# A hand-written planner's cost table and leads, re-measured and re-searched

## The chip, the cores and the metric

One core of one Trainium2 chip. Time is device microseconds of one execution; lower is better. The engines are TensorE (PE; PEld is its weight load), VectorE (DVE), ScalarE (ACT), GpSimd (POOL) and SyncE (SP, which only issues DMAs).

## The reference

Sorted block attention, whose output goes through a Fourier mixing layer with a normalised two-layer MLP. Four batches, 8 heads, 768 rows, 64 columns a head, 8 blocks of 96 rows; the model width is 512 and the MLP's is 2048.

```python
P = sort_net
for _ in range(5):                      # row and column normalisation of exp(P - max)
    ...
k_sorted = einsum('bhij,bhjcd->bhicd', P, k_blocks)     # v_sorted likewise
scores = scale * q_blocks @ k_sorted_blocks^T           # block by block
attn = softmax(scores); x = attn @ v_sorted             # (4, 768, 512)
X = real(fft(fft(x, axis=1), axis=2))
u = x + X
un = (u - mean(u)) / sqrt(var(u) + 1e-6)
out = u + relu(un @ w_ch1) @ w_ch2
```

## The kernel before

The work of one batch b runs through these steps; the names in quotes are those that the planner uses.

- Mixing of the blocks: "load_v" (SyncE) and "load_k16", "load_q16" (GpSimd) bring in a pair of heads. "psQ", "qT" turn q. "kron" makes the mixing matrix, "psK" and "kz" mix k. "psaT", "amr", "amr2", "psA", "a16", "a24" make the column means of v. "psV" mixes v, "vo" takes it from PSUM and subtracts the mean (VectorE, line 692, 8 to a batch), and "v_move" (line 700, 12 to a batch, SyncE) moves the mixed values with a DMA from one layout of partitions into another, `vs`. "a_out" and "a_row" move rows of means (lines 671 and 878).
- Attention, head by head: in batches 0 and 1 "psS" and "max" (line 771) find the maxima, "psT" and "exp" the shifted scores, "minus" takes 1 off in 16 bits, and "twice" (line 850) copies one column. In batches 2 and 3 the maxima come first along the other axis, and "turn_e" turns the result by a DMA. "psN" (line 856) multiplies by the values `vs`; it needs all moves of its half batch. "norm" (lines 862 and 863) divides on VectorE.
- Fourier transform: "fold" (line 882, VectorE or GpSimd) and "fold2" (line 887, VectorE, two instructions) add and subtract quarters of the rows for a pair of heads; "psWe", "psWo" (line 903) and the copies "We", "Wo" are the transform over the rows, "fold_d", "psF", "ot", "P", "Q" that over the columns.
- Sum and norm: "psR", "u", "add" (lines 1007 and 1008, GpSimd), "store_u" (line 1014, SyncE), "stats", "root", "nm", "un"; "psY" and "unT" turn the result on TensorE, or "turn_u" (line 1066) by a DMA in batches 2 and 3.
- MLP, two groups of 384 rows for each batch: "ph" (line 1104, four matmuls each), "relu" (line 1110), "pc" (line 1125, four matmuls each), "load_u" (line 1090, SyncE) brings back the residual, "outt" (line 1133) adds it, "store" (line 1148, GpSimd, indirect) writes the rows out.

Nothing on the chip chooses an order: each engine runs its own instructions in the order in which the program was written, and waits on semaphores. That order is made by the class `Plan` while the program is built. Each operation is a `step` with a duration in ns for every engine that can do it (`{"V": 425, "G": 1450}`), the keys that it reads and writes, and for a DMA its time on the queue (`work`) and until it has landed (`hop`). `run` keeps the list of steps whose predecessors are planned, works out for each when each engine could start it, takes all that could start within 40 ns of the earliest, and of these the one with the lowest priority number. A priority is 1e5 times the batch minus the length of the chain of steps still to come, plus a lead: `LEAD` gives for a step's name four numbers, one for each batch, in us (a negative one moves the step forward, a positive one back). The MLP's steps have priorities behind all of these, and bulk loads ahead of them.

Four of the planner's rules matter here. After a step the engine is taken to be free 60 ns before the step's end on VectorE and ScalarE (the last line of the `emit` part below). A step whose name is in `PORT` isn't started on VectorE while the planner has GpSimd at work, but 450 ns behind that at the latest. Whatever follows a DMA is put 2.5 us behind the time at which the planner has that DMA landed (`SPARE`). And a step that may run on two engines goes to the one that ends it sooner, if both have the same priority and could start within those 40 ns.

```python
        done = at + ns
        if e == "G" and not s.hop:
            self.pool = (at, done)
        self.free[e] = done if e in "TGS" else done - 60.0
```

Of the kernel before, what the change touches and what calls it, by code (L numbers as in the profile page):

```python
# [197 lines left out]
class Plan:  # L198
    HALF, TURNS = ("psQ", "psK", "psaT"), 200
    LAG, PE_TAIL, MARGIN, NEAR = 45.0, 215.0, 120.0, 40.0  # L200
    PORT, PORT_WAIT = ("fold", "fold_d", "minus", "nm", "un", "v_cast"), 450.0
    SPARE = 2500
    LEAD = dict(P=(42.1, 0, 0, 0), Q=(0, 32.3, 0, 0), We=(0, 0.1, 0, -4.3), Wo=(0, 0.1, 0, 0),
        a16=(0, 0, 0, 57.3), a24=(0, -25.2, 0, 0), add=(0, 0, 8.7, 0), amr2=(8.9, 0, 0, -13.1),
        exp=(0, 0, 17.5, 0), fold=(-32.4, 0, 41.2, -24.5), fold2=(-31.2, 0, 0, -34.7), kz=(1.7, 52.5, 0, 0),
        load_k16=(0, -3.8, -1.9, 0), load_q16=(0, -34.2, -1.6, -27.5), max=(54, 0, 0, 0),
        minus=(0, -8, 50.8, 3), psF=(30.4, 3.5, 0, 4.8), psK=(0, 0, 0, 15.9), psR=(7.6, 0, -10, 0),
        psS=(55.3, -5.2, 0, 0), psT=(5.1, -15.7, 0, 0), psWe=(0, 0, 0, 46.1), psY=(2.9, 0, 0, 0),
        psaT=(0, 7.5, 0, 0), stats=(-48, 2.1, 47.9, 0), twice=(0, 2.1, 0, -33.7), v_sum=(0, 0, -13.8, 0),
        vo=(0, -38.1, 0, -28.7))  # L210
    DMA_AHEAD = 800

    def __init__(self, engines):
# [179 lines left out]
def kernel(  # L393
# [108 lines left out]
    def load_v(b, hp, need):  # L502
        v32[b, hp] = Buf("hr" if 4 * b + hp in (0, 1, 2, 3, 7) else "v32")

        def f(e):
            nc.sync.dma_start(v_view(b, hp), v[b, 2 * hp:2 * hp + 2].rearrange(
                "h (p g) d -> p h (g d)", g=G))
# [160 lines left out]
    def a_out(b):  # L668
        def f(e):
            for p, lo, hi, at in ((BLK + 8, 0, 8, 0), (BLK + 9, 0, 7, 1), (BLK + 9, 7, 8, 4)):  # L670
                nc.sync.dma_start(xr2[b % 2][p:p + 1, lo:hi].rearrange("o i m -> o (i m)"),
                                  a16s[b % 2][at:at + hi - lo])
        step("a_out", b, {"S": 2100}, f, r=[("a16", b % 2)], w=[("xa", b % 2)], work=150, hop=1500, lanes=3)

    def row_zero(b):
        def f(e):
# [20 lines left out]
    def v_move(b, half):  # L697
        for g in range(G):
            def f(e, g=g):
                (nc.gpsimd if e == "G" else nc.sync).dma_start(  # L700
                    vs[2 * (b % 2) + half][16 * g:16 * g + 16].rearrange("c i e -> c (i e)"),
                    vo[half][:, g].rearrange("p h e -> p (h e)"))
# [93 lines left out]
    def turned(n):  # L796
# [22 lines left out]
        for y in range(2):  # L819
            es = Buf("es")  # L820

            def g(e, y=y, es=es):
# [6 lines left out]
            step("turn_e", b, {"S": 1250}, lambda e, y=y, es=es: nc.sync.dma_start(  # L829
                et.t[:, 4 * y:4 * y + 4, 0:BLK], es.t.rearrange("q j k -> q (j k)"), transpose=True),  # L830
                r=[es], w=[(et, y)], work=600, hop=1500)

# [11 lines left out]
    def values(n):  # L844
# [3 lines left out]
        def twice(e):  # L848
            row = eT[n].t[0:BLK].rearrange("p i q -> p (i q)")
            plan.engines[e].tensor_copy(row[:, BLK:NB * (BLK + 16):BLK + 17], eT[n].t[0:BLK, :, 0])  # L850
        step("twice", b, {"G": 270, "V": 120}, twice, r=[(eT[n], y) for y in range(2)], w=[(eT[n], 2)])

        def f(e):
            ps = pair(pN, D + 1, BLK + 8)
# [17 lines left out]
    def fold(b, hp):  # L872
# [5 lines left out]
        step("a_row", b, {"S": 600}, lambda e: nc.sync.dma_start(  # L878
            f2.t[BLK + 8:128, 0], a24[b % 2][:, None, ms].broadcast_to([24, 4, 128])),
            r=[("a24", b % 2)], w=[(f2, 0)], work=200, hop=1400)  # L880
        for y, op in enumerate(ops):
            step("fold", b, {"V": 425, "G": 1450}, lambda e, y=y, op=op: plan.engines[e].tensor_tensor(  # L882
                f1.t[:, y], xr[0:BLK + 8, 0:4, ms], xr[0:BLK + 8, 7:3:-1, ms], op=op), r=both, w=[(f1, y)])

        def f(e):
# [113 lines left out]
    def add_res(b, i, m):  # L999
# [4 lines left out]
        def f(e):  # L1004
# [4 lines left out]
        step("add", b, {"G": 1420}, f, r=[lo, hi, u], w=[u])  # L1009
# [49 lines left out]
    def transpose_u(b, i, m):  # L1059
# [3 lines left out]
        if (b, t // 4) not in unT:  # L1063
            unT[b, t // 4] = Buf("unT")
        if b >= 2 and (i, m) != (0, 1):
            step("turn_u", b, {"S": 1250}, lambda e: nc.sync.dma_start(
                unT[b, t // 4].t[:, :, BLK * (t % 4):BLK * (t % 4) + BLK],
                un[b, i, m].t[0:BLK], transpose=True),
                r=[un[b, i, m]], w=[(unT[b, t // 4], t % 4)], work=600, hop=1500)
# [13 lines left out]
    def mlp(b, gr):  # L1083
        hr, ur = {}, {}

        def load_u(t):
            q_ = 3 * gr + t
            ur[t] = Buf("ur")
            r0, r1 = 128 * q_, 128 * q_ + 128
            step("load_u", b, {"S": 430}, lambda e: nc.sync.dma_start(ur[t].t, u_dram[b][r0:r1]),  # L1090
                 r=[("ud", b, j) for j in range(8) if BLK * j < r1 and BLK * j + BLK > r0],
                 w=[ur[t]], work=800, hop=2000, prio=MLP - 1e8)
        MLP = 1e6 + 1e4 * b
# [44 lines left out]
    def store(b, q_, o, prio):  # L1138
        if (b, q_) == (B - 1, 5):
# [8 lines left out]
        step("store", b, {"G": 1020}, lambda e: nc.gpsimd.indirect_dma_start(  # L1148
            out=out.rearrange("b s m -> (b s) m"),
            out_offset=bass.IndirectOffsetOnAxis(ap=idx[:, c:c + 1], axis=0),  # L1150
            in_=o.t, in_offset=None), r=[o, "idx"], work=800, hop=1400, prio=prio)
# [17 lines left out]
        w.gates = (w1sb[0:1, 0, DM * c:DM * c + 1] if i < 4 else w2sb[0:1, 4 * c, 0:1])  # L1169

    def load_const(key, need, t, d):
        step("const", 0, {"S": 400}, lambda e: nc.sync.dma_start(t, d.ap()),
             w=[key], work=6 * int(np.prod(t.shape)) // 1000 + 50, hop=1500, bulk=t.shape[-1] > 1, need=need,
             rel=27000 if key in ("rsel", "idx") else 17500 if key in ("cdh",) else 0.0)

# [189 lines left out]
```

## Time and profile before

| | us |
|---|---|
| median of 3 runs | 324.42 |
| lowest and highest run | 320.97 and 324.87 |
| the profiled execution | 324.41 |
| its span | 322.6 |
| TensorE busy in the span | 285.3 |
| VectorE, ScalarE, GpSimd busy | 224.8, 203.4, 178.3 |

The granted TensorE clock was 0.974 of full speed in the mean. Matmuls are pipelined and their durations overlap, so a busy TensorE needn't be TensorE at its peak. In rows of a timeline stand the start, the length, the engine, the line and the operation with what it writes and reads; "x6" is that many instructions merged. The chain of waits is followed back from the last instruction to whatever released each piece. A wait is put down to what came last by the profile. "SPq" is the sequencer of SyncE, with the time that issuing a DMA takes there.

### The profile page before, as it was taken

How to read it: one execution, taken by the hardware profiler on the slowest of the kernel's cores; microseconds unless marked ns; L12 is line 12 of the kernel's file. 1: busy time of each engine (PE TensorE's matmuls, PEld its weight loads, DVE VectorE, ACT ScalarE, POOL GpSimd, SP SyncE). 2: the span in 40 equal slices, each digit the busy share in tenths (PEclk: the TensorE clock that was granted, in tenths of full speed). 3: DMA queues.
4: the chain of work that ended last, by engine and by line, in shares of the span. 5: the costliest groups of instructions: out<-in, count | busy, mean ns of one | idle time of the engine just before them, and what ended most of it. 6: DMA issues, size and time to landing. Idle time of an engine off the chain costs nothing.

```text
span 322.6 us, 7298 instructions
## 1 busy us (share of the span) xinstructions
PE 285.3 (88%) x2619; PEld 181.4 (56%) x2619; DVE 224.8 (70%) x487; ACT 203.4 (63%) x477; POOL 178.3 (55%) x246
## 2 busy tenths in 40 slices
PE   8877679959868798999999999997999999999990
PEld 5657556946655455555665656653655654645540
DVE  6689867899957989976878998998456764101010
ACT  6567657877746538875888989948832772713500
POOL 8623667849546799994748343975024965212020
PEclk9999966999989999999999999999999999999998
DMA  7952965897489977799997448556533537414021
GB/s 212 174 127 67 227 153 75 123 204 183 114 138 175 183 191 243 138 155 194 158 248 107 107 120 114 151 149 183 145 61 131 160 82 193 113 58 139 0 86 44
DMA packets 56062, 45.38 MB, mean 141 GB/s; under 512 B 25011, under 2 KB 48162, under 8 KB 56026
## 3 DMA queue, kind: packets, MB, share of 16 engines
q1 hardware_dynamic: 41226, 28.35, 34.7%
q0 software_dynamic: 14800, 16.57, 29.5%
q8 instruction: 20, 0.33, 0.4%
q14 instruction: 16, 0.13, 0.2%
HBM read 34.60 MB, written 12.58 MB: 146 GB/s over the span
## 4 chain that ended last, share of the span: by engine, by line
PE 49%; DVE 21%; DMA 12%; issue 6%; POOL 5%; SPq 3%; ACT 2%; POOLq 0%; DVEq 0%; ACTq 0%
PE bank L1104 18%; PE bank L1125 17%; DVE st L1025 3%; DMA vs<-vo 2%; PE bank L856 2%; DMA hr<-in_v_dram 2%; SPq L700 2%; DMA k<-in_k_dram 2%; DVE vo L692 2%; DMA out_dram<-outt,idx_sb 2%; DVE x L887 2%; DMA q<-in_q_dram 2%; PE bank L903 2%; DVE xr L863 2%; DVE kz L493 2%
## 5 line engine op out<-in xcount | busy, mean ns | idle before, releaser
L1104 PE MATMUL bank<-unT,w1sb 128*128 128x384 f16 x512 | 90.8, 328 | 2.2 <-DMA unT<-un 1.5
L1125 PE MATMUL bank<-w2sb,hr 128*128 128x512 f16 x384 | 90.6, 379 | 0.0
L1110 ACT ACTIVATE hr<-bank 128x384 f16<-128x384 f32 x128 | 60.7, 492 | 32.9 <-PE bank L1104 32.0
L1104 PEld LDWEIGHTS <-w1sb 128*128 128x128 f16 x512 | 48.5, 98 | 32.8 <-DMA unT<-un 2.0
L1125 PEld LDWEIGHTS <-hr 128*128 128x128 f16 x384 | 36.0, 98 | 37.5
L1148 POOL DMA_INDIRECT out_dram<-outt,idx_sb x23 | 23.7, 1028 | 55.1 <-DVE outt L1133 31.0
L1133 DVE SCALAR_TENSOR_TENSOR outt<-ur,bank 128x512 f32<-128x512 f32 x24 | 16.5, 686 | 37.9 <-PE bank L1125 37.4
L810 ACT ACTIVATE sm<-bank,mns 96x96 f32<-96x96 f32 x128 | 31.8, 344 | 2.3 <-DVE mns L815 2.2
L882 POOL TENSOR_TENSOR xs<-xr 104x512 f16<-104x512 f16 x13 | 16.1, 1239 | 18.8 <-DVE xr L863 14.0
L856 PE MATMUL bank<-vs,eT 97*104 97x65 f16 x256 | 17.4, 219 | 10.0 <-DMA vs<-vo 3.5
L1025 DVE BATCH_NORM_STATS2 st<-u 96x6 f32<-96x512 f32 (+1 forms) x32 | 21.7, 679 | 5.0 <-POOL u L1008 4.8
L856 PEld LDWEIGHTS <-eT 97*104 97x104 f16 x256 | 16.0, 135 | 14.3 <-issue 5.2
L863 DVE TENSOR_TENSOR xr<-bank,rz 104x512 f16<-104x512 f32 x32 | 22.1, 692 | 1.1
L1053 POOL TENSOR_SCALAR un<-u,mv,rstd 96x512 f16<-96x512 f32 (+1 forms) x8 | 17.0, 2125 | 10.3 <-PE bank L1076 4.1
L487 ACT COPY u<-bank 96x512 f32<-96x512 f32 (+1 forms) x24 | 13.5, 584 | 11.8 <-PE bank L984 6.8
L489 ACT ACTIVATE kz<-bank 64x768 f16<-64x768 f32 x20 | 16.1, 805 | 6.2 <-DVE kz L493 5.8
L887 DVE TENSOR_TENSOR x<-xs 104x512 f16<-104x512 f16 x32 | 16.9, 569 | 3.6 <-POOL xs L882 3.1
L487 ACT CAST W<-bank 128x384 f16<-128x384 f32 (+1 forms) x34 | 11.7, 383 | 10.2 <-PE bank L903 8.9
L815 DVE TENSOR_REDUCE mns<-bank 96x8 f32<-96x768 f32 x16 | 15.1, 946 | 2.0 <-PE bank L805 1.8
L903 PEld LDWEIGHTS <-x 128*128 128x128 f16 (+1 forms) x128 | 10.9, 103 | 9.7 <-DVE x L887 8.3
L692 DVE SCALAR_TENSOR_TENSOR vo<-a,bank 128x384 f16<-128x384 f16 x32 | 16.0, 539 | 0.0
L792 ACT ACTIVATE sm<-bank 96x768 f32<-96x768 f32 x16 | 12.8, 798 | 4.5 <-PE bank L787 4.0
(140 smaller groups left out, 538.6 us busy)
## 6 DMA issues: line engine op xcount, KB each, us to landing
u_dram<-u SPq DMA_DIRECT2D x32, 192.0 KB
ur<-u_dram SPq DMA_DIRECT2D x24, 256.0 KB
v<-in_v_dram SPq DMA_DIRECT2D x11, 384.0 KB
vs<-vo SPq DMA_DIRECT2D x48, 65.0 KB
k<-in_k_dram POOLq DMA_DIRECT2D x15, 192.0 KB, 4.3
q<-in_q_dram POOLq DMA_DIRECT2D x15, 192.0 KB, 5.7
w1sb<-in_moe_w_ch_dram POOLq DMA_DIRECT2D x4, 512.0 KB, 7.8
w2sb<-in_moe_w_ch_dram POOLq DMA_DIRECT2D x4, 512.0 KB, 5.9
```

What stands on the lines that cost most here:

```text
L487: nc.scalar.copy(dst, src)
L692: ("vo", b, {"V": 560}, lambda e: nc.vector.scalar_tensor_tensor(vo[h // 4][:, :, h % 4, 0:D], a16s[b % 2].rearrange("p (h d) -> p h d", d ...
L810: nc.scalar.activation(sm.t[:, i], pair(pS, BLK)[:, y, i % 4], AF.Exp, bias=mn.t[:, i:i + 1], scale=-1.0)
L856: nc.tensor.matmul(ps[:, i // 4, i % 4], eT[n].t[0:97, i, 0:BLK + 8], vs[2 * (b % 2) + h // 4][:, i, (D + 1) * (h % 4):(D + 1) * (h % 4 + 1)])
L863: nc.vector.tensor_tensor(xr2[b % 2][0:BLK + 8, :, D * h:D * (h + 1)].rearrange("p (t j) d -> p t j d", t=2), ps[:, :, :, 0:D], r[:, :, :, ...
L887: nc.vector.tensor_tensor(f2.t[0:BLK + 8, :, 2 * y:2 * y + 2].rearrange("p j f m -> p f j m"), f1.t[:, :, 0:2], f1.t[:, :, 3:1:-1], op=op)
L903: nc.tensor.matmul(ps[:, n * y:n * y + n], f2.t[r, j, xt[y], :], t[r, j, n * y:n * y + n], start=(y == 0 and j == 0), stop=(j == 1), skip_ ...
L1025: nc.vector.bn_stats(st.t[0:n], us[b, i, m].t[0:n])
L1104: nc.tensor.matmul(ps, w1sb[:, mc, 128 * fc:128 * fc + 128], unT[b, gr].t[:, mc, :], start=(mc == 0), stop=(mc == 3))
L1110: nc.scalar.activation(dst, bank(pH, [128, 384]), AF.Relu)
L1125: nc.tensor.matmul(ps, hr[f4].t[:, fc % 4, 128 * t:128 * (t + 1)], w2sb[:, fc, :], start=(fc == 0), stop=(fc == 15))
L1148: step("store", b, {"G": 1020}, lambda e: nc.gpsimd.indirect_dma_start(out=out.rearrange("b s m -> (b s) m"), out_offset=bass.IndirectOffs ...
```

## The change

Only numbers of the planner change, and one rule of it; the operations are the same.

- Durations on SyncE: load_v 400 to 520, a_out 2100 to 2300, v_move 600 to 645, turn_e 1250 to 1300, a_row 600 to 920, store_u 350 to 550, turn_u 1250 to 1310, load_u 430 to 600, constants 400 to 450 ns.
- Durations on GpSimd: twice 270 to 200, fold 1450 to 1160, add 1420 to 1380, store 1020 to 1050 ns.
- The overlap of successive operations, 60 ns for both, becomes 80 on VectorE and 100 on ScalarE.
- fold2 and twice join `PORT`.
- All leads are new.

```diff
-    PORT, PORT_WAIT = ("fold", "fold_d", "minus", "nm", "un", "v_cast"), 450.0
+    PORT, PORT_WAIT = ("fold", "fold2", "twice", "fold_d", "minus", "nm", "un", "v_cast"), 450.0
+    OVER = {"V": 80, "A": 100}
     SPARE = 2500
-    LEAD = dict(P=(42.1, 0, 0, 0), Q=(0, 32.3, 0, 0), We=(0, 0.1, 0, -4.3), Wo=(0, 0.1, 0, 0),
-        a16=(0, 0, 0, 57.3), a24=(0, -25.2, 0, 0), add=(0, 0, 8.7, 0), amr2=(8.9, 0, 0, -13.1),
-        exp=(0, 0, 17.5, 0), fold=(-32.4, 0, 41.2, -24.5), fold2=(-31.2, 0, 0, -34.7), kz=(1.7, 52.5, 0, 0),
-        load_k16=(0, -3.8, -1.9, 0), load_q16=(0, -34.2, -1.6, -27.5), max=(54, 0, 0, 0),
-        minus=(0, -8, 50.8, 3), psF=(30.4, 3.5, 0, 4.8), psK=(0, 0, 0, 15.9), psR=(7.6, 0, -10, 0),
-        psS=(55.3, -5.2, 0, 0), psT=(5.1, -15.7, 0, 0), psWe=(0, 0, 0, 46.1), psY=(2.9, 0, 0, 0),
-        psaT=(0, 7.5, 0, 0), stats=(-48, 2.1, 47.9, 0), twice=(0, 2.1, 0, -33.7), v_sum=(0, 0, -13.8, 0),
-        vo=(0, -38.1, 0, -28.7))
+    LEAD = dict(We=(0, 0, 0, -32.4), Wo=(-26.1, 0, -22, 0), a_row=(0, -15.8, -6.7, -8.5), amr=(0, 0, 0, -24.3),
+        exp=(0, 0, 0, -11.5), fold=(0, -20.3, 0, -26.8), fold2=(0, 0, 0, -6.4), fold_d=(0, 0, -41.8, 0),
+        load_k16=(0, 6, 9.2, 1.9), load_q16=(0, 2.4, 9, 0), load_v=(0, 0, 0, 20.2), max=(0, -0.7, 0, 0),
+        minus=(0, 0, -9.8, -5.4), norm=(60, 0, 0, 0), psR=(0, 14.5, -4.4, 0), psT=(-12.2, 52.1, 0, 0),
+        psV=(0, 0, 0, -14.1), psWo=(-0.9, 0, 0, -20.5), psY=(0, 0, -15.5, 0), stats=(-5, 53.1, 0, 26.5),
+        twice=(14.6, 0, 0, 0), unT=(0, 0, -12.4, 0), v_move=(0, 0, 0, -12.9), vo=(0, 0, -36.6, 0),
+        weights=(-7.7, 0, 0, 0))
...
-        self.free[e] = done if e in "TGS" else done - 60.0
+        self.free[e] = done - self.OVER.get(e, 0.0)
...
-        step("load_v", b, {"S": 400}, f, w=[v32[b, hp]], work=1250, hop=1450, bulk=True, need=need, rel=80000 if b == 2 else 27000 if b == 1 else 0.0)
+        step("load_v", b, {"S": 520}, f, w=[v32[b, hp]], work=1250, hop=1450, bulk=True, need=need, rel=80000 if b == 2 else 27000 if b == 1 else 0.0)
...
-            step("v_move", b, {"S": 600}, f,
+            step("v_move", b, {"S": 645}, f,
...
-        step("a_row", b, {"S": 600}, lambda e: nc.sync.dma_start(
+        step("a_row", b, {"S": 920}, lambda e: nc.sync.dma_start(
...
-            step("fold", b, {"V": 425, "G": 1450}, lambda e, y=y, op=op: plan.engines[e].tensor_tensor(
+            step("fold", b, {"V": 425, "G": 1160}, lambda e, y=y, op=op: plan.engines[e].tensor_tensor(
...
-        step("store_u", b, {"S": 350}, lambda e: nc.sync.dma_start(
+        step("store_u", b, {"S": 550}, lambda e: nc.sync.dma_start(
...
```

More of the change, by code (lines that the diff above doesn't have):

```diff
@@ L672, in f @@
                                   a16s[b % 2][at:at + hi - lo])
-        step("a_out", b, {"S": 2100}, f, r=[("a16", b % 2)], w=[("xa", b % 2)], work=150, hop=1500, lanes=3)
+        step("a_out", b, {"S": 2300}, f, r=[("a16", b % 2)], w=[("xa", b % 2)], work=150, hop=1500, lanes=3)
     def row_zero(b):
@@ L828, in turned @@
             step("minus", b, {"V": 385, "A": 518}, g, r=[(sm, y)], w=[es])
-            step("turn_e", b, {"S": 1250}, lambda e, y=y, es=es: nc.sync.dma_start(
+            step("turn_e", b, {"S": 1300}, lambda e, y=y, es=es: nc.sync.dma_start(
                 et.t[:, 4 * y:4 * y + 4, 0:BLK], es.t.rearrange("q j k -> q (j k)"), transpose=True),
@@ L850, in twice @@
             plan.engines[e].tensor_copy(row[:, BLK:NB * (BLK + 16):BLK + 17], eT[n].t[0:BLK, :, 0])
-        step("twice", b, {"G": 270, "V": 120}, twice, r=[(eT[n], y) for y in range(2)], w=[(eT[n], 2)])
+        step("twice", b, {"G": 200, "V": 120}, twice, r=[(eT[n], y) for y in range(2)], w=[(eT[n], 2)])
         def f(e):
@@ L1008, in f @@
             eng.tensor_tensor(u.t[0:n, LH:DM], u.t[0:n, LH:DM], h[0:n, 255:0:-1], op=ALU.add)
-        step("add", b, {"G": 1420}, f, r=[lo, hi, u], w=[u])
+        step("add", b, {"G": 1380}, f, r=[lo, hi, u], w=[u])
     def store_u(b, i, m):
@@ L1065, in transpose_u @@
         if b >= 2 and (i, m) != (0, 1):
-            step("turn_u", b, {"S": 1250}, lambda e: nc.sync.dma_start(
+            step("turn_u", b, {"S": 1310}, lambda e: nc.sync.dma_start(
                 unT[b, t // 4].t[:, :, BLK * (t % 4):BLK * (t % 4) + BLK],
@@ L1089, in load_u @@
             r0, r1 = 128 * q_, 128 * q_ + 128
-            step("load_u", b, {"S": 430}, lambda e: nc.sync.dma_start(ur[t].t, u_dram[b][r0:r1]),
+            step("load_u", b, {"S": 600}, lambda e: nc.sync.dma_start(ur[t].t, u_dram[b][r0:r1]),
                  r=[("ud", b, j) for j in range(8) if BLK * j < r1 and BLK * j + BLK > r0],
@@ L1147, in store @@
         c = 6 * b + q_
-        step("store", b, {"G": 1020}, lambda e: nc.gpsimd.indirect_dma_start(
+        step("store", b, {"G": 1050}, lambda e: nc.gpsimd.indirect_dma_start(
             out=out.rearrange("b s m -> (b s) m"),
@@ L1171, in load_const @@
     def load_const(key, need, t, d):
-        step("const", 0, {"S": 400}, lambda e: nc.sync.dma_start(t, d.ap()),
+        step("const", 0, {"S": 450}, lambda e: nc.sync.dma_start(t, d.ap()),
              w=[key], work=6 * int(np.prod(t.shape)) // 1000 + 50, hop=1500, bulk=t.shape[-1] > 1, need=need,
```

## The prediction

> **What bounds the kernel now.** I read the page first: the span, the busy shares, the slices and the chain.
>
> ```profile
> span 322.6 us, 7298 instructions
> PE 285.3 (88%) x2619; PEld 181.4 (56%) x2619; DVE 224.8 (70%) x487; ACT 203.4 (63%) x477; POOL 178.3 (55%) x246
> PE   8877679959868798999999999997999999999990
> PEclk9999966999989999999999999999999999999998
> ```
>
> The profiled execution took 324.41 us, 1.8 us more than its span, and the median of the three runs is 324.42 us; I sum against 324.4. TensorE is the busiest engine, and the slices show two regimes: up to about 110 us it has holes and, in two places, a lower clock; behind that it is nearly full. Stages of the windows view make that exact (columns: stage, length, busy time and count of PE, PEld, DVE, ACT, POOL, then granted clock, DMA share, GB/s).
>
> ```profile
> 40.00:42.00 2.00, 0.00 (x0) 0.00 (x0) 0.45 (x2) 0.00 (x0) 2.00 (x2) 1.00 1.11 260
> 43.50:53.50 10.00, 9.74 (x87) 6.78 (x86) 8.55 (x17) 7.55 (x14) 6.31 (x8) 0.51 0.49 69
> 60.00:83.00 23.00, 18.30 (x245) 14.07 (x243) 22.74 (x50) 18.16 (x35) 17.27 (x22) 1.00 0.84 170
> 83.00:307.00 224.00, 211.88 (x1727) 127.15 (x1726) 153.34 (x325) 145.72 (x383) 123.39 (x163) 0.99 0.64 141
> 94.00:98.00 4.00, 4.00 (x35) 3.13 (x34) 3.22 (x7) 2.14 (x3) 4.00 (x4) 0.57 0.69 78
> 220.00:230.00 10.00, 8.47 (x67) 5.38 (x66) 6.13 (x15) 7.66 (x27) 3.47 (x3) 1.00 0.73 204
> ```
>
> From 43.5 to 53.5 us TensorE ran at 0.51, from 94 to 98 at 0.57. From 60 to 83 VectorE is the bound, 22.74 of 23 us. Behind 83 TensorE is busy 211.88 of 224 us, 94.6%: what is won or lost before that point reaches the end at about 0.95. The two dips stand right behind TensorE's two longest single waits. The waits view (total, count, longest), then GpSimd's wait between 88 and 95 us (its L1159 reads what L700 moves) and a row of the timeline:
>
> ```profile
> PE bank L903 <- DVE x L887: 3.8, 8, 1.0
> PE bank L856 <- DMA vs<-vo: 3.5, 1, 3.5
> PE bank L856 <- issue: 3.2, 1, 3.2
> PE bank L1104 <- DMA unT<-un: 1.5, 1, 1.5
> POOL landed L1159 <- DMA vs<-vo: 4.0, 1, 4.0
> 93.45 0.54 PE L856 MATMUL bank<-vs,eT 97*104 97x65 f16 x8 [3.18 <-issue]
> ```
>
> Both are the same thing: the value matmul (L856) stands at the head of TensorE's fixed order while the last v_move (L700) of its batch is still under way. The second wait is called "issue", but GpSimd's wait for the same move ends at the same 93.45. The wait of 1.5 us for unT (within 220 to 230 us) left the clock at 1.00. The chain of waits shows how the first comes about:
>
> ```profile
> 23.21 3.73 DVE vo L692 x8
> 27.38 0.61 SPq L700
> 35.20 7.14 DMA vs<-vo
> 42.39 0.59 PE bank L856 x8
> ```
>
> **The change part by part.** No instruction is added or removed; the planner's durations, overlaps, port rule and priorities change, so the same operations come in another order, and some on another engine.
>
> *SyncE's durations.* SP's rows around both moves:
>
> ```profile
> 24.00 2.60 SPq L878 DMA_DIRECT2D x<-a  x3
> 26.70 3.86 SPq L700 DMA_DIRECT2D vs<-vo  x6
> 30.60 0.59 SPq L506 DMA_DIRECT2D v<-in_v_dram  x1
> 31.30 2.48 SPq L700 DMA_DIRECT2D vs<-vo  x4
> 33.82 0.74 SPq L506 DMA_DIRECT2D v<-in_v_dram  x1
> 34.61 1.90 SPq L700 DMA_DIRECT2D vs<-vo  x2
> 76.24 0.62 SPq L700 DMA_DIRECT2D vs<-vo  x1
> 86.14 1.83 SPq L700 DMA_DIRECT2D vs<-vo  x3
> ```
>
> Three a_row, twelve v_move and two load_v took from 24.00 to 36.51: 12.51 us. The old numbers give 3 x 0.60 + 12 x 0.60 + 2 x 0.40 = 9.8, the new 3 x 0.92 + 12 x 0.645 + 2 x 0.52 = 11.54. So the planner believed the moves 2.7 us too early and will be 1.0 too early: 1.7 us of the 3.49 us wait is now seen in advance, and other matmuls can be put ahead of L856. I take **A = -1.7** (0 to -3.5: nothing at hand to fill, or the wait gone). For batch 1, twelve v_move and four store_u lie between 76.24 and 87.97, 11.73 us; old 12 x 0.60 + 4 x 0.35 = 8.6, new 12 x 0.645 + 4 x 0.55 = 9.94. **C = -1.3** of 3.2 (0 to -3.2). load_u, turn_e, turn_u, const and a_out issue behind 60 us or in SP's idle time, where SP ends no TensorE wait but unT's 1.5; I put them at 0, covered by MLP matmuls; without that cover 1.5 at most, either way.
>
> *The half clock.* In the stage at 0.51 the chain of waits from 42.39 to 54.00 is half TensorE:
>
> ```profile
> by line: DVE x L887 18.4%; DVE xr L863 17.9%; PE bank L903 16.5%; PE bank L987 7.4%; PE bank L991 7.4%; PE bank L984 7.3%; PE bank L740 6.7%; PE bank L856 5.1%; DVE W L491 4.9%; ACT W L487 4.3%; DVE rz L862 3.9%; issue 2.0%; DVE eT L850 1.6
> ```
>
> The PE shares make 50.4% of 11.6 us, 5.85 us, and at full clock half of that. A wait of 3.49 - 1.7 = 1.8 us is nearer to the 1.5 that kept the clock than to the 3.2 that lost it. **B = -2.9** (0 to -2.9). From 94 to 98 the loss is 4 x (1 - 0.57) = 1.7; the wait left there would be 1.9, a closer thing, so I take half: **D = -0.9** (0 to -1.7).
> [...]
>
> *PORT, OVER and GpSimd's durations.* fold2 (L887) and twice now wait in the plan for GpSimd to finish, as fold did.
>
> ```profile
> L887 DVE TENSOR_TENSOR x<-xs x32: 408/425/1611, 37.3 to 245.4; 104x512 f16<-104x512 f16 x32
> L887 DVE TENSOR_TENSOR x<-xs 104x512 f16<-104x512 f16 x32 | 16.9, 569 | 3.6 <-POOL xs L882 3.1
> 45.70 2.21 DVE L887 TENSOR_TENSOR x<-xs 104x512 f16<-104x512 f16 x2
> 106.43 1.69 DVE L887 TENSOR_TENSOR x<-xs 104x512 f16<-104x512 f16 x2
> L882 DVE TENSOR_TENSOR xs<-xr x19: 409/426/1355, 35.8 to 243.6; 104x512 f16<-104x512 f16 x19
> L882 POOL TENSOR_TENSOR xs<-xr x13: 1140/1166/1387, 40.0 to 243.7; 104x512 f16<-104x512 f16 x13
> 23.14 3.79 DVE L692 SCALAR_TENSOR_TENSOR vo<-a,bank 128x384 f16<-128x384 f16 x8
> 26.85 5.26 DVE L771 TENSOR_REDUCE mxs<-bank 96x8 f16<-96x768 f32 x6
> L692 DVE SCALAR_TENSOR_TENSOR vo<-a,bank 128x384 f16<-128x384 f16 x32 | 16.0, 539 | 0.0
> ```
>
> At the median a pair takes 0.85; these two lost 1.4 and 0.8 us, 2.2 together, the first where L887 leads the chain (the row above). The rule helps only where another VectorE operation is ready: **E = -1.0** (+1.0, idling for GpSimd in vain, to -2.2). OVER is right: eight vo of 539 ns would be 4.31 us and took 3.79, 75 ns less at each joint; old 60, new 80. That is 20 ns on 487 operations, in the planner's book only; 0. A fold on GpSimd counted 1450 and took 1166, now 1160: more folds go there. Each takes 0.43 us off VectorE and ends its own chain 0.74 later; between -0.4 and +0.7 for one, I take 0, as DVE is full from 60 to 83 and the fold's followers wait elsewhere (L903 for L887, 3.8 us). add, store and twice move by 30 to 70 ns: 0.
>
> *The leads.* In batch 0 the maxima (max, psS) lose a delay of some 55 us, norm gets one of 60; batch 1's vo loses an advance of 38.1, and psT gets a delay of 52.1. In batch 0 all eight vo went ahead of six maxima. SP began to move at 26.70 with the fourth vo done at about 25.0 (23.14 + 3.79/2), so two maxima (5.26/6 = 0.88 each) ahead cost 0.1, four 1.9, none 0; I take 0, as the maxima must be done anyway before L856 can run. norm's delay sets it behind whatever else is ready in batch 0: at most one maximum for each of four pairs of heads, 3.5 either way, as the same maxima are then early; 0. The rest of the leads falls mostly behind 83 us, where TensorE idles 12.1 us: that is the most they can win, with MLP matmuls as cover, and without that cover a loss of a wait like those two, 3.5; 0. Batch 1's vo is the third rival.
>
> Sum: -1.7 - 2.9 - 1.3 - 0.9 - 1.0 = -7.8, of which 0.946 (211.88/224) reaches the end, -7.4: 324.4 - 7.4 = **317.0 us**. All terms at their far ends give -13.5 x 0.946 = -12.8 (311.6); at their near ends +1 and the leads' +1.9.
>
> **The rivals.** *The wait isn't SP's, but the transfer's* (same). The last v_move was issued by 36.51 and landed at 42.39; 5.9 us pass behind SP, while the DMA engines are full (share 1.11 from 40 to 42 us, 260 GB/s). The change leaves the planner's transfer times alone. Then A, B, C and D fall to about a fifth, -1.4, and with E the time is 324.4 - 2.4 x 0.946 = 322.1. For it: the long landing; against: the old plan was wrong about SP's part too.
> *The clock comes back by itself.* If a dip lasts one short stretch wherever it falls, as the second did, and the waits only get shorter, B and D give nothing: -4.0 x 0.946, 320.6. Against it stands the first dip's 10 us. [...]
> *Batch 1's values come later* (slower). vo has lost its 38.1 us advance, and VectorE is full there:
>
> ```profile
> 70.64 1.01 DVE L692 SCALAR_TENSOR_TENSOR vo<-a,bank 128x384 f16<-128x384 f16 x2
> 79.08 0.95 DVE L771 TENSOR_REDUCE mxs<-bank 96x8 f16<-96x768 f32 x1
> ```
>
> Four more maxima of 0.95 ahead of the last vo put the moves 3.8 us later, the wait at L856 goes from 3.2 to 7.0, and the dip lasts 10 us like the first instead of 4, another 3.0: 324.4 + 6.8 = 331.2. It decides from about 3.5 us of lateness on, if no MLP matmuls of batch 0 are put ahead of L856. For it: that order is fixed in advance, and the old one had two maxima between the vo's; against: batch 0's MLP offers matmuls.
>
> **How the numbers follow.** Forecast, some gain in both waits and the dips: 0.42, its own range 311 to 318. Transfer: 0.18. Clock: 0.12. Batch 1 late: 0.28; further lateness of that sort adds to it, so its tail is long. Two per cent, 6.5 us, is about what a measurement of this kernel can tell from no change: faster (under 317.9) 0.42, same 0.30, slower (over 330.9) 0.28. The range is 310 to 333: it leaves out the slow tail, some 0.15, and a little below.
>
> **What would show it.** A: L856's first wait for vs at 2 us or less. B: no stage at 0.5 between 40 and 60 us. C and D: the same between 85 and 100. E: L887 under 500 ns in the mean (569 now would be unchanged). Rival one: both waits over 3 us. Rival two: shorter waits, dips of 4 us or less, time near 320. Rival three: batch 1's last vo behind 83 us, and L856 waiting 5 us or more. The prediction is wrong if the holes before 110 us only move elsewhere: then TensorE's busy time stays at 285 us and the span with it.

## The result, and the profile after

The changed kernel takes 317.92 us, the median of four runs (316.6 to 319.2); the kernel before, run beside it, 323.25 (four runs, 320.97 to 324.87). The ratio is 0.987, with a 95% interval of 0.982 to 0.992: 1.3% faster, where 2.3% was forecast, so the gain is real but lies inside the 2% called "the same". The profiled execution took 317.89 us, against 324.41 before; these two are 6.5 us apart, the medians 5.3, and 1.3% is 4.1. Executions of one program differed by up to 3.4% from each other (the kernel before took 318.0 to 328.89 us beside the second running of the changed one), and the ratios here and below leave out those over 1.5% above the fastest of their kernel.

The page of the changed kernel, its span, busy shares and slices:

```profile
span 316.1 us, 7297 instructions
PE 284.5 (90%) x2619; PEld 185.4 (59%) x2619; DVE 220.8 (70%) x476; ACT 201.3 (64%) x480; POOL 178.3 (56%) x254
PE   8878588858989998899999999999999999999990
PEclk9999978996699999999999999999999999999997
```

TensorE does the same 2619 matmuls in nearly the same busy time (284.5 for 285.3 us); the span is 6.5 us shorter. Only 0.8 of that is busy time, so 5.7 us of holes are gone. (A matmul at half clock counts as busy for its longer time, so this counts holes, not work: in the kernel before one of L984, 105x512, took 631 ns from 43.5 to 53.5 us at a clock of 0.51 and 381 from 110 to 300 at 1.00.) Where they were is seen in the windows view, by stages that cover the whole span. First three stages of the kernel before (columns as in the prediction: stage, length, busy time of PE, PEld, DVE, ACT, POOL, clock, DMA share, GB/s):

```profile
0.00:83.00 83.00, 65.95 (x860) 51.02 (x861) 69.37 (x160) 57.66 (x95) 52.39 (x80) 0.94 0.76 153
83.00:116.00 33.00, 26.36 (x253) 17.33 (x252) 26.06 (x56) 17.78 (x36) 21.75 (x31) 0.95 0.82 157
210.00:250.00 40.00, 36.54 (x258) 21.11 (x257) 28.04 (x60) 21.55 (x63) 15.27 (x17) 1.00 0.52 134
```

The same view of the changed kernel, with the two dips of before and a new one below:

```profile
0.00:83.00 83.00, 65.20 (x859) 53.38 (x860) 68.73 (x157) 53.31 (x88) 55.71 (x82) 0.90 0.78 160
83.00:116.00 33.00, 30.88 (x290) 20.50 (x290) 29.90 (x62) 23.62 (x50) 26.26 (x38) 0.99 0.81 165
210.00:250.00 40.00, 39.77 (x297) 24.44 (x296) 29.49 (x69) 24.59 (x71) 19.49 (x26) 1.00 0.52 140
...
40.00:42.00 2.00, 2.00 (x21) 1.93 (x20) 0.28 (x1) 0.83 (x2) 1.46 (x2) 0.50 1.24 251
43.50:53.50 10.00, 7.44 (x108) 6.22 (x105) 9.80 (x17) 8.08 (x13) 8.57 (x12) 0.83 0.69 105
74.00:84.00 10.00, 9.76 (x94) 7.72 (x90) 7.94 (x18) 7.28 (x14) 8.71 (x10) 0.50 0.66 185
94.00:98.00 4.00, 4.00 (x36) 2.93 (x34) 3.67 (x10) 3.52 (x10) 3.36 (x5) 1.00 1.07 153
83.00:307.00 224.00, 218.35 (x1757) 131.77 (x1757) 151.38 (x320) 148.03 (x393) 121.97 (x171) 1.00 0.62 141
```

Up to 83 us nothing was won: TensorE idles 17.8 us instead of 17.05 and its clock is 0.90 instead of 0.94. From 83 to 116 it is busy 4.5 us longer, from 210 to 250 another 3.2. The stage between, 116 to 130, gives 1.6 back (11.53 busy instead of 13.11). That makes 2.9 us won around 83 to 130, 3.2 from 210 to 250, and little elsewhere: 5.7 in all. Behind 83 us TensorE is busy 97.5% (218.35 of 224), 94.6% before.

The longest waits of TensorE (total, count, longest):

```profile
PE bank L856 <- DMA vs<-vo: 2.1, 1, 2.1
PE bank L768 <- DVE kz L493: 2.1, 1, 2.1
```

In the timeline, the row of the first value matmul, and GpSimd's copy that reads what batch 1's moves have written:

```profile
39.17 0.56 PE L856 MATMUL bank<-vs,eT 97*104 97x65 f16 x8 [2.11 <-DMA vs<-vo]
91.66 0.18 POOL L1159 COPY landed<-vs 96x1 f16<-96x1 f16 x1
```

The first wait for `vs` has gone from 3.49 to 2.11 us. The second, 3.18 us before, is gone: the copy `landed` has no wait any more. But a wait of 2.1 us for a VectorE copy (kz) stands at 66 us, where there was none of that length.

### The profile page after: what moved, and what is told of

Read it like the earlier page. It is cut to its first block, busy times and chain, and to the rows that moved or that the text cites. A ratio compares the mean times of both kernels' runs of the same rounds, so it can differ in the third digit from the quotient of the medians.

```text
span 316.1 us, 7297 instructions
## 1 busy us (share of the span) xinstructions
PE 284.5 (90%) x2619; PEld 185.4 (59%) x2619; DVE 220.8 (70%) x476; ACT 201.3 (64%) x480; POOL 178.3 (56%) x254
## 4 chain that ended last, share of the span: by engine, by line
PE 47%; DVE 18%; POOL 9%; DMA 9%; issue 7%; ACT 5%; SPq 2%; POOLq 0%; DVEq 0%; ACTq 0%
PE bank L1125 18%; PE bank L1104 18%; DMA out_dram<-outt,idx_sb 3%; DMA q<-in_q_dram 2%; DVE st L1025 2%; DVE vo L692 2%; SPq L700 2%; DMA vs<-vo 2%; PE bank L856 2%; ACT kz L489 2%; POOL v L533 2%; PE bank L903 2%; POOL u L1008 2%; DVE kz L493 1%; DVE x L887 1%
## 5 line engine op out<-in xcount | busy, mean ns | idle before, releaser
L1104 PE MATMUL bank<-unT,w1sb 128*128 128x384 f16 x512 | 89.7, 326 | 0.5 <-DVE xr L863 0.3
L1104 PEld LDWEIGHTS <-w1sb 128*128 128x128 f16 x512 | 48.9, 98 | 32.3 <-issue 1.9
L1148 POOL DMA_INDIRECT out_dram<-outt,idx_sb x23 | 24.5, 1064 | 60.9 <-DVE outt L1133 26.5
L882 POOL TENSOR_TENSOR xs<-xr 104x512 f16<-104x512 f16 x15 | 18.4, 1228 | 14.9 <-DVE xr L863 12.5
L856 PE MATMUL bank<-vs,eT 97*104 97x65 f16 x256 | 17.8, 220 | 4.4 <-DMA vs<-vo 2.1
L856 PEld LDWEIGHTS <-eT 97*104 97x104 f16 x256 | 16.9, 138 | 7.5 <-issue 3.1
L1007 POOL TENSOR_TENSOR u<-u,P 96x257 f32<-96x257 f32 (+1 forms) x16 | 11.6, 728 | 13.3 <-DVE P L965 7.8
L487 ACT CAST W<-bank 128x384 f16<-128x384 f32 (+1 forms) x33 | 10.9, 374 | 11.1 <-PE bank L903 10.4
L487 ACT COPY u<-bank 96x512 f32<-96x512 f32 (+1 forms) x18 | 10.4, 586 | 11.2 <-PE bank L984 7.4
L850 POOL COPY eT<-eT 96x8 f16<-96x8 f16 x25 | 6.8, 278 | 18.0 <-ACT eT L839 11.3
L887 DVE TENSOR_TENSOR x<-xs 104x512 f16<-104x512 f16 x32 | 14.5, 492 | 1.5 <-POOL xs L882 1.0
```

Of the source, the lines that this page charges most:

```text
L487: nc.scalar.copy(dst, src)
L856: nc.tensor.matmul(ps[:, i // 4, i % 4], eT[n].t[0:97, i, 0:BLK + 8], vs[2 * (b % 2) + h // 4][:, i, (D + 1) * (h % 4):(D + 1) * (h % 4 + 1)])
L882: step("fold", b, {"V": 425, "G": 1160}, lambda e, y=y, op=op: plan.engines[e].tensor_tensor(f1.t[:, y], xr[0:BLK + 8, 0:4, ms], xr[0:BLK ...
L1104: nc.tensor.matmul(ps, w1sb[:, mc, 128 * fc:128 * fc + 128], unT[b, gr].t[:, mc, :], start=(mc == 0), stop=(mc == 3))
L1148: step("store", b, {"G": 1050}, lambda e: nc.gpsimd.indirect_dma_start(out=out.rearrange("b s m -> (b s) m"), out_offset=bass.IndirectOffs ...
```

## The experiments

Each kernel is compared with runs of the kernel before beside it on the same chip; the first four shared these, then the next three, the next four and the last.

**The two halves of the change.** One kernel takes the durations, the overlaps and the port rule, with the old leads:

```diff
-    LEAD = dict(We=(0, 0, 0, -32.4), Wo=(-26.1, 0, -22, 0), a_row=(0, -15.8, -6.7, -8.5), amr=(0, 0, 0, -24.3),
...
+    LEAD = dict(P=(42.1, 0, 0, 0), Q=(0, 32.3, 0, 0), We=(0, 0.1, 0, -4.3), Wo=(0, 0.1, 0, 0),
...
```

> All of the change but the leads: new durations, new overlaps, fold2 and twice in the port rule, with the leads of before. If the truer table by itself makes the better order, the time is near 318 to 320 us and L856's wait for the first move is near 2 us. If the gain is in the leads, searched for this very table, the old leads don't fit it: 322 to 330 us, with holes before 130 us as before.

The other takes the new leads with the old numbers and rule:

```diff
-    PORT, PORT_WAIT = ("fold", "fold2", "twice", "fold_d", "minus", "nm", "un", "v_cast"), 450.0
+    PORT, PORT_WAIT = ("fold", "fold_d", "minus", "nm", "un", "v_cast"), 450.0
-        self.free[e] = done - self.OVER.get(e, 0.0)
+        self.free[e] = done if e in "TGS" else done - 60.0
-            step("v_move", b, {"S": 645}, f,
+            step("v_move", b, {"S": 600}, f,
...
```

> The new leads alone, on the old table. If the leads carry the gain by themselves (maxima earlier in batch 0, mixing of batch 1 not held back), 318 to 321 us. If leads and table only work together, about 324 us or more, up to 335, since the old table puts steps elsewhere than where the leads were searched.

Both are slower than the kernel before: the table alone 1.024 (1.018 to 1.031), 328.9 us; the leads alone 1.028 (1.022 to 1.035), 330.7 us. The table alone has its first wait for the moves down to 1.9 us, as a truer price of SP's work should give, and no waits from 210 to 250 us; but it loses from 190 to 210 us, with a clock of 0.83 there. The leads alone have the old waits for the moves, and longer:

```profile
190.00:210.00 20.00, 16.11 (x134) 10.30 (x133) 17.57 (x39) 14.64 (x41) 10.83 (x16) 0.83 0.44 113
```

```profile
PE bank L855 <- DMA vs<-vo: 7.3, 2, 3.7
```

The halves don't add: +2.4% and +2.8% make -1.3% together. Truer durations were worth nothing by themselves here. Leads fit the table that they were found with, and go off when it changes.

**Batch 3's leads.** The changed kernel, with batch 3's column of the leads as before:

```diff
-    LEAD = dict(We=(0, 0, 0, -32.4), Wo=(-26.1, 0, -22, 0), a_row=(0, -15.8, -6.7, -8.5), amr=(0, 0, 0, -24.3),
...
+    LEAD = dict(We=(0, 0, 0, -4.3), Wo=(-26.1, 0, -22, 0), a16=(0, 0, 0, 57.3), a_row=(0, -15.8, -6.7, 0),
...
```

> The changed kernel with batch 3's leads of before; the planner's order is the same up to about 160 us. If the 3 us that TensorE no longer idles between 210 and 250 us come from batch 3's leads, the time rises by 2 to 4 us to 320 to 322, the waits at 210 to 250 come back and everything before 160 us is unchanged. If they come from the table (turn_u and turn_e issued as priced) or from the head start alone, the time stays within 1 us of 318.

It took 0.991 of the time before (0.987 to 0.996), 319.8 us. From 210 to 250 TensorE is busy 39.56 us, so the holes did not come back: batch 3's leads alone don't explain the 3.2 us. The difference to the changed kernel is between nothing and 2 us, not resolved.

**The port rule.** The changed kernel without fold2 and twice in `PORT`:

```diff
-    PORT, PORT_WAIT = ("fold", "fold2", "twice", "fold_d", "minus", "nm", "un", "v_cast"), 450.0
+    PORT, PORT_WAIT = ("fold", "fold_d", "minus", "nm", "un", "v_cast"), 450.0
```

> The changed kernel without fold2 and twice in the port rule; the order is the same up to about 42 us. If the rule is worth what my term E says, the mean of L887 goes back from 492 to about 570 ns and the time rises by 1 us, to 319. If it only moved the order about, L887's mean rises but the time stays at 318 or moves by several us for other reasons, which the waits before 130 us would show.

The ratio is 0.991 (0.985 to 0.996), not to be told from the changed kernel's. The group of fold2 in the changed kernel, then in this one (busy time, mean of one in ns, idle before it):

```profile
L887 DVE TENSOR_TENSOR x<-xs 104x512 f16<-104x512 f16 x32 | 14.5, 492 | 1.5 <-POOL xs L882 1.0
```

```profile
L887 DVE TENSOR_TENSOR x<-xs 104x512 f16<-104x512 f16 x32 | 13.4, 458 | 0.8 <-POOL xs L882 0.6
```

Fold2 went from 569 to 492 ns in the mean, and without the rule it is 458 (in a profiled execution of 326.71 us; this kernel's median is 320.96). With the new leads alone, without the rule, it is 497; with the table and the rule but the old leads, 422. So the rule is not needed for the 492: the order of work by itself moves fold2 as much. What the rule is worth in a fixed order was not tried.

**What the half clock costs.** Dummy matmuls (128x386, into a bank that is written over afterwards) are put into TensorE's waits, so that it should not idle there. In the kernel before, ahead of the value matmuls of two heads:

```diff
+    def fill(p, count):
+        for _ in range(count):
+            nc.tensor.matmul(p.t[:, 0, 0:386], ident, cse[:, 0])
...
+            fill(pN, {4: 20, 12: 18}.get(n, 0))
```

> The kernel before, with matmuls of no use (128x386, results overwritten) in TensorE's two long waits: 20 ahead of the fifth head's value matmuls of batch 0, 18 ahead of those of batch 1. The order is untouched. If the half clock costs what terms B and D say, both stages at half clock go and the time falls by 2.5 to 4.5 us, to 319 to 321. If the clock's dips cost nothing because VectorE bounds those stages, the clock is full and the time stays within 1 us of 323.3. If the dips don't come from these waits, they stay.

In the changed kernel, in the same way with 12, 12 and 6:

```diff
+            fill(pS, {12: 12}.get(n, 0))
...
+            fill(pS, {12: 6}.get(n, 0))
...
+            fill(pN, {4: 12}.get(n, 0))
```

> The changed kernel with such matmuls in its waits: 12 ahead of the fifth head's value matmuls of batch 0, 12 ahead of the maxima's matmuls of head 12 and 6 ahead of the score matmuls of head 12, where it waits about 2, 2 and 1 us. If waits of 2 us bring the dips, those from 39 to 49 us and from 74 to 84 us go or shorten, and the time falls by 1 to 4 us if the half clock is on the path there, by under 1 us if VectorE bounds.

Before, filled: 1.004 (1.000 to 1.008), no gain. Its stage of the first dip and the one behind it:

```profile
42.00:53.50 11.50, 8.96 (x133) 6.47 (x131) 10.11 (x20) 9.39 (x17) 7.59 (x11) 1.00 0.63 111
...
54.00:62.00 8.00, 7.74 (x87) 6.95 (x88) 5.17 (x9) 4.42 (x8) 5.31 (x9) 0.59 0.61 89
```

The dip from 43.5 to 53.5 is gone, the clock is 1.00. TensorE then is busy only 8.96 of 11.5 us, and its waits for VectorE's fold2 come to 5.8 us in all instead of 3.8. VectorE works 10.11 of 11.5 us: it is the next bound of this stage, and at full clock TensorE waits longer for it. But the stage does get shorter. The order is the same in both kernels, so the same operations can be set side by side: two maxima right behind the stage and the next two, in the kernel before and in the filled one (there L771 is L775, L856 is L861 and L984 is L989).

```profile
55.94 1.81 DVE L771 TENSOR_REDUCE mxs<-bank 96x8 f16<-96x768 f32 x2
60.52 1.82 DVE L771 TENSOR_REDUCE mxs<-bank 96x8 f16<-96x768 f32 x2
```

```profile
54.63 1.81 DVE L775 TENSOR_REDUCE mxs<-bank 96x8 f16<-96x768 f32 x2
61.41 1.82 DVE L775 TENSOR_REDUCE mxs<-bank 96x8 f16<-96x768 f32 x2 [0.75 <-PE bank L772]
```

At full clock 1.31 us are won; then the filled kernel's own dip, from about 54 to 60.5 us, puts it 0.89 us behind. At the second place TensorE goes on at 93.52 us instead of 93.45, at a clock of 1.00 from 88 to 96, and some eight us later the same matmul starts 1.51 us earlier, before and filled:

```profile
101.53 0.38 PE L984 MATMUL bank<-xr,rsel_sb 105*97 105x512 f16 x1 [0.82 <-DVE xr L863]
```

```profile
100.02 0.38 PE L989 MATMUL bank<-xr,rsel_sb 105*97 105x512 f16 x1 [0.82 <-DVE xr L868]
```

That lead lasts until another dip at 221 us; at the end 0.7 us of it is left (span 321.9 for 322.6). So each of the two dips did cost time, 1.3 and 1.5 us. Filling two waits let other dips come elsewhere, and the time of the whole kernel did not fall.

The changed kernel, filled: 0.994 (0.989 to 1.000), if anything slower than without. In the profiled execution the filling worked:

```profile
0.00:83.00 83.00, 64.45 (x890) 51.70 (x891) 69.22 (x157) 54.16 (x89) 55.30 (x82) 0.99 0.77 157
```

A clock of 0.99 up to 83 us instead of 0.90 left the span at 316.2 us (316.1 without). That is not the price of the dips, for the added matmuls take time of their own. Those meant for the wait for kz came to stand behind it:

```profile
68.80 2.12 PE L755 MATMUL bank<-cse_sb,ident 128*128 128x386 f16 x12 [2.10 <-DVE kz L493]
```

In most of its twelve executions the filling did not work: their median clock was 0.961, as without it. The three with a clock of 0.98 or more took 317.9 to 318.6 us, the other nine 320.1 to 325.7. What the dip from 74 to 84 costs is better read from the kernel of new-then-old order below, which has the changed kernel's order up to there, nothing added, and no dip there (clock 1.00). Two of VectorE's operations, in the changed kernel and in that one:

```profile
72.16 0.18 DVE L1026 BATCH_NORM_AGGREGATE mv<-st 96x2 f32<-96x6 f32 x1
82.35 0.69 DVE L863 TENSOR_TENSOR xr<-bank,rz 104x512 f16<-104x512 f32 x1
```

```profile
71.74 0.18 DVE L1161 BATCH_NORM_AGGREGATE mv<-st 96x2 f32<-96x6 f32 x1
80.29 0.69 DVE L998 TENSOR_TENSOR xr<-bank,rz 104x512 f16<-104x512 f32 x1
```

It is 0.42 us ahead at the first and 2.06 at the second: 1.6 us for this dip, of which 1.2 are left at 88 us. Over the 206 executions of the experiments, the time within one kernel falls by 1.6 us for each 0.01 of mean clock (correlation -0.64). That doesn't say which causes which: the wait of 3.18 us in the kernel before is idle time itself, and has the dip to 0.57 behind it. So at three places, in one execution each, a dip cost 1.3 to 1.6 us. That is less than B's 2.9 for the first and more than D's 0.9 for the second.

**SP's order alone.** In the kernel before, two a_row of batch 0 are issued behind the twelve v_move, whose landing should come earlier:

```diff
+                moves.append(g)
+                if len(moves) == 12:
+                    for row in held:
+                        row()
...
-        step("a_row", b, {"S": 600}, lambda e: nc.sync.dma_start(
+        step("a_row", b, {"S": 600}, lambda e: held.append(row) if b == 0 and hp in (1, 2) else row(),
```

> The kernel before with one thing moved, on SyncE alone: the a_row of the second and third pair of heads, of batch 0, are issued behind the twelve v_move instead of ahead. If SyncE's issuing ends the first wait, the moves start 1.6 us earlier, land at about 40.8, and L856 waits 1.9 us instead of 3.5; the time falls by 1.5 us, by up to 4 if the half clock goes with it. If the transfer itself ends it, the landing stays at 42 and so does the time.

0.999 (0.995 to 1.003). The last move was issued by 35.12 us instead of 36.51, and the value matmul (here L861) started at 41.34 instead of 42.39:

```profile
41.34 1.91 PE L861 MATMUL bank<-vs,eT 97*104 97x65 f16 x22 [3.83 <-DMA hr<-in_v_dram]
```

It waited 3.83 us all the same, as TensorE too had reached it earlier. (The view names another DMA as the end of the wait; what the matmul reads is `vs`.) One us is 0.3% of the time, too little for the ratio to tell. The trace keeps most of it: the two maxima at 55.94 us start at 55.20 here, the matmul at 101.53 at 100.73, and the span is 321.4 us for 322.6.

**The changed kernel again, and two orders joined.** The changed kernel unchanged, on another chip:

> The changed kernel again, on the chip and in the rounds of the next three, as their measure: 0.987 of the kernel before, about 318 us.

0.990 (0.985 to 0.995), 317.8 us: the result repeats. Three kernels then run one program's order up to a point of the plan and the other's from there on (each engine's order is written out as a list, `ORDER`, and the steps are taken from it). The changed order up to 104 us of the plan, the old one behind:

```diff
+ORDER = """
+3A13400 24T13620 0A13885 27T14165 2V14200 25V14540 1A14584 173G14665 26A14874 18T15139 28V15410 29A15564
...
+"""
```

> The order of the changed kernel for all steps that its plan starts before 104 us (about 116 us in the trace), then the order of the kernel before for the rest. TensorE's work done is 3.3 us ahead at 116 us and falls behind nowhere later; if that is a gain for good, 1 per cent, about 320 us. If it was only borrowed, and the old order from there on waits for the same things at the same time, 323 us.

The reverse, with the same edit and the other list, cut at 104 and at 172 us:

> The reverse: the order before for what its plan starts before 104 us, then the new order. If the 4 us between 210 and 250 us are the new order's own, 319 to 320 us; if they only come from being early, about 323; if the new order needs its own beginning, 325 or more.

> The order before up to 172 us of its plan (about 190 us in the trace), then the new one. In the old order the moves of batch 3's values stand on SyncE right ahead of the turns that the second MLP group of batch 2 waits for; with the switch made as late as this, the moves of batch 3 that the old plan starts from 179 us on come in the new order, right away. If that is where the 4 us come from, TensorE no longer waits 1.5 us for unT and the time is 319 to 321 us; if it comes from the order of batch 3's mixing, which is planned before 172 us in the new order, it stays at 323 us or above.

New, then old: 0.996 (0.991 to 1.002), 320.0 us, 2.2 us behind the changed kernel beside it. Old, then new: 1.000 (0.994 to 1.006), 321.7 us. Cut later: 1.022 (1.012 to 1.033), 327.2 us. Here are the stages from 210 to 250 of new-then-old and of old-then-new (39.77 in the changed kernel):

```profile
210.00:250.00 40.00, 35.80 (x257) 21.49 (x256) 25.52 (x58) 22.41 (x67) 16.33 (x19) 1.00 0.50 133
```

```profile
210.00:250.00 40.00, 39.77 (x296) 23.99 (x295) 30.51 (x68) 25.35 (x77) 19.00 (x24) 1.00 0.55 139
```

The 3.2 us from 210 to 250 belong to the second part of the order: with the old second part the holes are there (35.80), with the new one they are not (39.77), whatever went before. Joined the other way that gain is lost again at the seam: from 116 to 130 us TensorE is busy 12.05 us at a clock of 0.76, and the later seam opens a wait of its own (line numbers here are 135 higher than in the kernel before):

```profile
PE bank L1122 <- DMA xr<-xr: 4.6, 1, 4.6
```

**The kernel before again.** Without an edit, to see whether the second wait belongs to the program or to one execution, and what the comparison gives for no change:

> The kernel before, profiled once more. Two later kernels with its very order up to 104 us of the plan had no wait for batch 1's moves. If that wait of 3.2 us, and the dip behind it, belonged to the one execution that the prediction was read from, it is absent here, the profiled execution takes 321 to 322 us instead of 324.4, and the first wait and the holes between 210 and 250 us are there as before. If it belongs to the program, it is there again and the time is near 324. The ratio to the kernel before is 1.000 and shows what the rounds can tell.

1.005 (1.000 to 1.009): a difference under about 1% can't be told here. The second wait is there again, and so is the late landing of the first moves:

```profile
42.34 2.29 PE L856 MATMUL bank<-vs,eT 97*104 97x65 f16 x24 [2.14 <-DMA vs<-vo]
...
94.23 0.87 PE L856 MATMUL bank<-vs,eT 97*104 97x65 f16 x8 [3.15 <-issue]
```

The first value matmul starts at 42.34 us, as before (42.39), after a wait of 2.14 us instead of 3.49. TensorE came to it later, since the clock was halved from about 35 us on already (0.50 from 36 to 42). Those 7 us at half clock cost nothing: TensorE would only have waited longer for the moves.

## Why the prediction was right or wrong

The time came out 0.9 us above the forecast and in its range, but not by the forecast's steps: a large term failed, others were too small, and these nearly balance. That it came so near is luck, helped by the start: the forecast counts down from 324.4, while the kernel before had a median of 323.25 beside the changed one. Of a forecast gain of 7.4 us, 4.1 (by the ratio) to 5.3 (by the medians) came.

**A, the first wait: right in size, by another way, without an effect.** It was to shrink by 1.7 us, as other matmuls are put ahead of L856, and shrank by 1.4. But TensorE reaches L856 1.8 us earlier than before (37.06 for 38.90 us), and the moves land 3.2 us earlier (39.17 for 42.39). SP's rows in the changed kernel, and the end of the wait in the chain:

```profile
23.29 1.73 SPq L878 DMA_DIRECT2D x<-a  x2
25.82 3.21 SPq L700 DMA_DIRECT2D vs<-vo  x5
29.07 0.60 SPq L506 DMA_DIRECT2D v<-in_v_dram  x1
29.73 4.41 SPq L700 DMA_DIRECT2D vs<-vo  x7
34.18 0.84 SPq L878 DMA_DIRECT2D x<-a  x1
```

```profile
33.54 5.50 DMA vs<-vo
```

One a_row and one load_v have gone behind the moves, which are done at 34.14 us instead of 36.51; the landing comes 5.0 us behind that (5.9 before). That part of rival one, a long landing that the plan doesn't know, is true and stays. But the 1.4 us don't reach the end. TensorE's idle time up to 83 us grew by 0.8, since other waits stand there now (kz, 2.1). The step that failed is "what is won or lost before that point reaches the end at about 0.95". Where the order is kept, most of a shorter wait is carried on: with SP's order alone the landing comes 1.05 us earlier, and 0.74 of it is left at 56 us, 0.80 at 101. In the changed kernel, with another order, other waits and another dip took the place of the 1.4.

**B, the half clock: failed.** "A wait of 3.49 - 1.7 = 1.8 us is nearer to the 1.5 that kept the clock than to the 3.2 that lost it." The wait left was 2.11 us, and the clock is at 0.50 right behind it (40 to 42 us). From 43.5 to 53.5 it was indeed 0.83 instead of 0.51, but a new dip of 10 us stands from 74 to 84. And the filled kernel shows that the second half of the step was too large: half of the PE shares of the chain, 2.9 us, was the price, and full clock won 1.3 us, since VectorE, busy 8.55 of those 10 us already, is the next bound there. Across all executions the clock didn't change: the median is 0.959 over 102 of the kernel before and 0.962 over 16 of the changed one. By the slope above the difference would be 0.4 us (0.0025 before rounding) of the 4 to 5 won. Rival two, that the dips give nothing, was right about the changed kernel's time up to 83 us and wrong in its reason: there is no less half clock than before (0.90 for 0.94), only elsewhere, again with a stretch of 10 us, and such a stretch has a price (1.6 us from 74 to 84). The five stretches of half clock ahead of the last matmuls, in the traces of before and after, were these: 10.24 us from 43.1 and 3.41 from 94.3 before; 3.41 from 39.6, 3.41 from 46.4 and 10.24 from 73.7 after. In the two long ones the clock was 0.50 although TensorE was busy for 9.98 and 10.00 of the 10.24 us.

**C, the second wait: too small, with another cause.** 1.3 of 3.2 us were to go, all went. SP's durations can't be the only reason, for the old order joined to the new one has no such wait either, with the same issues. In the kernel before, the last three moves, GpSimd's 512 KB load of `w2` beside them and the copy that waits for the moves:

```profile
86.14 1.83 SPq L700 DMA_DIRECT2D vs<-vo  x3
86.50 0.85 POOL L1165 DMA_DIRECT2D w2sb<-in_moe_w_ch_dram  x1
93.45 0.19 POOL L1159 COPY landed<-vs 96x1 f16<-96x1 f16 x1 [4.02 <-DMA vs<-vo]
```

The same three in the kernel of old order with the late seam, which has the old order here:

```profile
85.59 1.83 SPq L835 DMA_DIRECT2D vs<-vo  x3
87.39 0.85 POOL L1300 DMA_DIRECT2D w2sb<-in_moe_w_ch_dram  x1
90.28 0.38 POOL L1294 COPY landed<-vs 96x1 f16<-96x1 f16 x1
```

| kernel | load starts ahead of the moves' end by | landing behind that end | wait of TensorE |
|---|---|---|---|
| SP's order alone | 1.74 us | 5.7 us | 3.6 us |
| before | 1.47 | 5.5 | 3.2 |
| before again | 1.25 | 5.7 | 3.15 |
| before, filled | 0.83 | 4.2 | filled by the added matmuls |
| old, then new | 0.63 | at most 2.3 | none |
| old, then new, late | 0.03 | at most 2.9 | none |

With the load issued over 1.2 us ahead, the moves land some 3 us later; with 0.83 us, 1.3 to 1.9 later; with 0.63 or less they don't. In the changed kernel batch 1's moves end at 80.34 and the load starts at 84.35. So the wait reads as a collision of transfers, which rival one had in mind, and it fell away as the moves moved 7.6 us forward. That the load is the cause is argued from six executions; no kernel that moves the load alone was tried.

**D: right.** The clock from 94 to 98 is 1.00, as the wait before it is gone. The filled kernel puts the price of that dip at 1.5 us (0.9 was taken, up to 1.7). In the changed kernel the dip from 74 to 84 costs as much again.

**E: the right number for a wrong reason.** Fold2 came under 500 ns (492; 77 ns by 32 is 2.5 us of VectorE). Without the rule it is 458, so the rule is not shown to be the cause.

**The leads and the turns, put at 0: too small.** "The rest of the leads falls mostly behind 83 us", where TensorE's idle time "is the most they can win"; 0 was chosen between that and a loss, and the turns were put at 1.5 at most. From 210 to 250 alone 3.2 us were won. In the kernel before SP issues the turns of `un` late, behind batch 3's moves; TensorE waits for one:

```profile
218.53 1.27 SPq L1066 DMA_TRANSPOSE unT<-un  x1
```

This is the third turn. In the changed kernel the moves come earlier and the turns with them, the third at:

```profile
213.40 1.20 SPq L1066 DMA_TRANSPOSE unT<-un  x1
```

It is issued 5.1 us earlier, and no wait over 0.2 us is left in this stage (1.5, 0.7, 0.5, 0.4 and 0.4 before). Whether leads or table do it isn't settled. It is not batch 3's leads alone, and the kernel with the new table and the old leads is full from 210 to 250 us too (40.00 us busy), though it idles 3.9 us from 190 to 210.

**Rival three, batch 1's values later: wrong in direction.** The last vo of batch 1 ends at about 75 us instead of 79.2. It lost its advance of 38.1 us, but in the same batch the delays of kz (52.5) and Q (32.3) went as well, which may be why it came earlier all the same; only the first was weighed, and none was tried alone.

The account on the profiled executions: A and B were to give 4.4 at the end and gave nothing (idle time up to 83 us +0.8); C and D were to give 2.1, and their stage, 83 to 130, gave 2.9; the leads and the turns were to give 0, and 210 to 250 gave 3.2; E's and other small changes make up the rest of 6.5. The split goes by stages: that 83 to 130 is C and D alone is not shown. The last sign named in the prediction, a busy time that stays at 285 us and a span that stays with it, was badly chosen: the busy time did stay (284.5), as the matmuls are the same, and the span fell, since it is idle time that went.

## What to carry to other kernels

Before a wait or a slow clock is priced, ask in that stage which engine comes next: where VectorE works 10 of 11.5 us, a full clock on TensorE won 1.3 us, not half of TensorE's 5.85. To price it, set the same operation of two executions with one order side by side; the whole time also holds the dips that came elsewhere. Priorities found by a search belong to the cost table they were found with; a better table without a new search, or the leads without the table, was over 2% slower here. A late small transfer is read with everything that other queues issue in the few microseconds around it, not by its own queue alone: here the last move landed 5.5 us behind its issue where a 512 KB load had been issued 1.47 us ahead of that point, and at most 2.3 us where it was 0.63.

## What was not expected of the hardware

- A wait's length didn't settle what the clock did behind it. After 2.11 us it was halved at once in the changed kernel (0.50 from 40 to 42 us), after the 2.10 us for kz there it stayed at 1.00 from 68 to 73, and after the same 2.10 us in new-then-old order it was 0.57 from 68 to 72. Two dips lasted 10 us (0.51 from 43.5 to 53.5 before, 0.50 from 74 to 84 after) although TensorE was busy 97% of that time.
- The same half clock had very different prices: nothing for 7 us ahead of the moves' landing, 1.5 us for 3.4 us from 94 us on.
- Where the dips fell varied between executions of one program: the first began at about 43 us in one execution of the kernel before and at 35 in another, and its mean clock lay between 0.934 and 0.979.
- The landing of the last 65 KB move took 5.5 to 5.7 us behind its issue with a 512 KB load issued over 1.2 us ahead of that point, 4.2 us with 0.83 us, and 2.3 to 2.9 us at most with 0.63 us or less.
